# Loads of k and q issued two slots ahead, and GpSimd's last sums of w_a put behind VectorE's last sums of h

## The chip, the cores and the metric

The kernel runs on one core of one Trainium2 chip. The metric is the time of one execution on the device, in microseconds (us). Three runs of the kernel before took 219.48, 219.63 and 220.11 us; their median is 219.63 us.

## What is computed

Four batches of eight heads go through a decayed linear recurrence over 768 steps with heads of width 64, and its output, seen as 3072 tokens of width 512, goes through a bilinear feed-forward layer of width 1536:

```python
for t in range(S):
    state = gamma * state + einsum('bhd,bhe->bhde', k[:, :, t], v[:, :, t])
    y[:, :, t] = scale * einsum('bhd,bhde->bhe', q[:, :, t], state)
x = y.transpose(0, 2, 1, 3).reshape(B * S, H * D)
out = ((x @ w_a) * (x @ w_b)) @ w_out
```

Inputs and output are float32; the kernel multiplies in bf16 and sums in float32.

## The kernel before, in words

**Slots and blocks.** The 24 slots (four batches of six) are 128 steps each. For a slot, k and q are multiplied by tables of decays into one bf16 tile `kqb` (`scaled`, line 233), a DMA turns that tile over into `kqT` (line 256), and v is cast to bf16 into `vb` (line 264). From these, `turn` (line 411) makes on TensorE the state sums of two slots (`chunk_states`, line 281), their scores (`scores`, line 315) and the outputs of the two slots before (`inter`, `intra`), which ScalarE or VectorE copies into `xt`, the input of the feed-forward layer. The 3072 tokens go through that layer in eight blocks J of 4, 2, 2, 2, 2, 4, 4 and 4 slots (`TILES`, line 16). For each of twelve stripes `ft` of the width of 1536, TensorE makes a (`ffn_a`) and g (`ffn_g`), ScalarE copies a to bf16 (line 606), and VectorE multiplies the two into `ht` (line 617).

**Products with seven multiplications.** The product with w_out in J of 2 to 7 is made of seven products of halves where eight would be plain (`ffn_fast`, line 779, once for every two slots, so u = 0 and 1 in a block of four). It needs sums of parts of h, `hsum`, which `add` (line 664) makes: for each pair of stripes f four sums, numbered `which` 0 to 3. VectorE makes most of them. In J = 6 and 7 the product with w_a has this form as well, for f from 1 on (`seven_a`, line 719), and so needs sums of parts of x, `xs` (`combine_x`, line 678, on VectorE), and sums of parts of w_a, `ta` (`combine_a`, line 687, on GpSimd: four instructions for each f). In J = 6 the seven multiplications serve f of 1 to 3, in J = 7 f of 1 to 5. In J = 6 GpSimd also makes the sums of h of f up to 3 (`sums_of`, line 996), and VectorE those of f = 4 and 5 (`adds_of`), the last seven of them behind the last `ht`.

**Banks.** PSUM has three banks that a, g, the state sums and the products o share (`psff`, line 67). In `ffn_fast` the products R1, R2, R4 and R5 take banks from these three. R2 goes into the output by `plus` (line 791) on VectorE, and that instruction sets its bank free. Behind the three that R1, R2 and R4 hold, the state sums of a `turn` take the bank of R4, and R5 that of R2.

**Order of the work.** On every engine the order is that of the program: `seq` (line 75) ties each instruction to the one before it on its engine. What interleaves the slots with the blocks is a table written by hand, `ahead` (line 951): at the point (J, ft), (J, "o", i), (J, "mid") or (J, "sums", u) it calls `casts`, `turn` or `combine_a`, and `visit` (line 972) runs what stands there. Slots 6 to 23 go through `casts` (line 250): on GpSimd the two products with the tables and the cast of v, on SyncE's DMA queue (SP) the turning over and the loads that follow. SP issues DMAs one after the other, and one that waits holds up those behind it. The raw tiles of k, q and v hold two slots each and there are three of each kind; of `kqb`, `kqT` and `vb` there are six, so slot t takes over the tiles of slot t - 6. `store` (line 629) issues the outputs on SP, too. `combine_a` for f = 1, 2, 3 stands at (5, "sums", 0) behind the casts of slot 23, and for f = 4 and 5 in `sums_of` behind GpSimd's sums of h of J = 6, f = 3.

Of the kernel before, what the change touches and what calls it, by code (L numbers as in the profile page):

```python
# [12 lines left out]
ALU = mybir.AluOpType  # L13
# [14 lines left out]
def kernel(  # L28
# [10 lines left out]
    nc = tc.nc  # L39
# [8 lines left out]
    NSLOT = B * NCH  # L48
# [23 lines left out]
    last = {}  # L72
    nosync = mybir.DependencyInfo(mybir.DependencyClass.NoSync, mybir.DependencyReason.DATA)

    def seq(bi):
        ins = bi.ins
        prev = last.get(ins.engine)
        if prev is not None:
            tc.add_manual_dep(ins, prev.name, nosync, reason="program order")
        last[ins.engine] = ins  # L80
        return bi
# [4 lines left out]
    def load_slot(t, names="kqv"):  # L86
        b, ci = divmod(t, NCH)
        for nm in names:
            if t % 2 == 0:
                whole[nm] = raw.tile([P, 2, H, D], F32, tag=nm + "f", name=nm + "f")  # L90
            raws[nm, t] = whole[nm][:, t % 2]
            s = {"k": k, "q": q, "v": v}[nm][b, :, ci * P : (ci + 1) * P, :]
            if nm == "q":
                s = s.rearrange("h (n par) d -> par n h d", par=2)
                for par in range(2):
                    seq(nc.sync.dma_start(out=raws[nm, t][64 * par : 64 * par + 64], in_=s[par]))
            else:
                seq(nc.sync.dma_start(out=raws[nm, t], in_=s.rearrange("h p d -> p h d")))
# [101 lines left out]
    def cast(engine, dst, src):  # L200
        if engine is nc.scalar:
            seq(nc.scalar.copy(dst, src))  # L202
        else:
            seq(engine.tensor_copy(dst, src))  # L204
# [28 lines left out]
    def scaled(eng, t, i):  # L233
        ktab, qtab = tabs[0] if t < 2 * PAIRS else tabs[1]
        dst, src, tab = kqb[t][:, i], raws["kq"[i], t], (ktab, qtab)[i][:, t % NCH]
        dst = dst.rearrange("p hp r d -> p r hp d")
        src = src.rearrange("p (r hp) d -> p r hp d", r=2)
        tab = tab.rearrange("p (r hp) o -> p r hp o", r=2).to_broadcast([P, 2, HP, D])
        if t < 10:
            seq(eng.tensor_tensor(dst, src, tab, op=ALU.mult))  # L240
        else:
            for r in range(2):
                seq(eng.tensor_tensor(dst[:, r], src[:, r], tab[:, r], op=ALU.mult))  # L243

    def new_nat(t):
        kqb[t] = nat.tile([P, 2, HP, 2, D], BF16, tag="kqb", name="kqb")
        kb[t], qb[t] = kqb[t][:, 0], kqb[t][:, 1]
        vb[t] = nat.tile([P, H, D], BF16, tag="vb", name="vb")

    def casts(t, names="kqv"):  # L250
        if "k" in names:
            new_nat(t)
            scaled(nc.gpsimd, t, 0)
            scaled(nc.gpsimd, t, 1)
            kqT[t] = tra.tile([P, 2, HP, P], BF16, tag="kqT", name="kqT", bufs=6)
            seq(nc.sync.dma_start_transpose(
                out=kqT[t].rearrange("p a b c -> p (a b) c"),
                in_=kqb[t].rearrange("p a hp r d -> p (a hp r d)")))
            if t % 2 and t + 1 < NSLOT:
                for names in ("kq", "v"):  # L260
                    load_slot(t + 1, names)
                    load_slot(t + 2, names)
        if "v" in names:
            cast(nc.gpsimd, vb[t], raws["v", t])

# [13 lines left out]
    sums = {}  # L279
# [54 lines left out]
    after = mybir.DependencyInfo(mybir.DependencyClass.Sync, mybir.DependencyReason.DATA)  # L334
# [329 lines left out]
    def add(J, which, f0, f1, eng=nc.vector):  # L664
        if J not in hsum:
            hsum[J] = [wstage.tile([P, NH, 2, P], BF16, tag="w" + "ab"[i % 2], name="hsum") for i in range(4)]
        s = [x[:, f0:f1, : TILES[J] // 2] for x in hsum[J]]
        x, y, op = {
            0: (lambda: rows(J, 0, 1, f0, f1), lambda: rows(J, 1, 1, f0, f1), ALU.add),
            1: (lambda: s[0], lambda: rows(J, 0, 0, f0, f1), ALU.subtract),  # L670
            2: (lambda: rows(J, 0, 0, f0, f1), lambda: rows(J, 0, 1, f0, f1), ALU.subtract),
            3: (lambda: rows(J, 1, 0, f0, f1), lambda: s[1], ALU.subtract),
        }[which]
        seq(eng.tensor_tensor(s[which], x(), y(), op=op))  # L674
# [12 lines left out]
    def combine_a(f):  # L687
        if not ta:
            ta.extend(raw.tile([P, 2, NH, P], BF16, tag=t, name="ta") for t in ("kf", "kf", "qf", "qf"))
        w = wa_bf.rearrange("p (c k) (f r m) -> p c r f k m", c=2, r=2, m=P)  # L690
        b11, b12, b21, b22 = (w[:, c, r, f] for c in range(2) for r in range(2))
        t1, t2, t3, t4 = (t[:, :, f] for t in ta)
        for dst, x, y in ((t1, b12, b11), (t2, b22, t1), (t3, b22, b12), (t4, b21, t2)):
            seq(nc.gpsimd.tensor_tensor(dst, x, y, op=ALU.subtract))

    banks = {}

# [61 lines left out]
    behind = []  # L759
# [189 lines left out]
    for j in range(NO):  # L949
        cast_o(j)  # L950
    ahead = {
        (1, 6): [(casts, 6)], (1, 8): [(casts, 7)],
        (0, "o", 2): [(turn, 6, None), (casts, 8, "kq")],
        (0, "o", 3): [(casts, 9, "kq"), (casts, 8, "v"), (casts, 9, "v")],
        (1, "o", 1): [(turn, 8, 6, D_), (casts, 10)],
        (2, 2): [(casts, 11)], (2, 7): [(casts, 12)], (2, "o", 0): [(turn, 10, 8), (casts, 13)],
# [3 lines left out]
        (5, 0): [(casts, 20)], (5, 2): [(casts, 21)], (5, 3): [(turn, 16, None)],  # L960
        (5, 8): [(turn, 18, 16), (casts, 22)],
        (5, "sums", 0): [(turn, 20, 18), (casts, 23)],
        (6, 8): [(turn, 22, 20)], (6, "o", 0): [(turn, None, 22)],
    }
    ahead[5, "sums", 0] += [(combine_a, f) for f in (1, 2, 3)]
    early = {3: [(0, 0, 2)], 4: [(1, 0, 2)], 5: [(2, 0, 2)], 6: [(3, 0, 2)],
             7: [(0, 2, 4)], 8: [(1, 2, 4)], 9: [(2, 2, 4)], 10: [(3, 2, 4)]}
# [14 lines left out]
    def blocks_seven(J):  # L982
        f0, f1 = SEVEN[J]
        combine_x(J)
        store()
        for ft in range(2 * f0):
            ffn_a(J, ft)
        for f in range(f0, f1):
            seven_a(J, f)
            sums_of(J, f - 1)  # L990
            mask_now(1)
        seven_end(J, f1 - 1)
        sums_of(J, f1 - 1)
        return 2 * f1

    def sums_of(J, f):
        if J == 6 and f == 0:
            return
        if J == 6:
            f0, f1 = (0, 2) if f == 1 else (f, f + 1)  # L1000
            for which in range(4):
                add(J, which, f0, f1, nc.gpsimd)
            if f == 3:
                combine_a(4)
                combine_a(5)
        elif f < 5:
            for which in range(4 if f < 4 else 2):
                add(J, which, f, f + 1, nc.gpsimd)
        else:
            for which in range(2):  # L1010
                add(J, which, 5, 6)
            for which in (2, 3):
                add(J, which, 4, 6)
# [61 lines left out]
```

## Time and profile before

| | |
|---|---|
| median of three runs | 219.63 us |
| the profiled execution | 220.27 us |
| its span, first to last instruction | 218.6 us |
| TensorE busy | 211.2 us, 97% of the span |
| VectorE busy | 147.0 us, 67% |
| GpSimd busy | 120.7 us, 55% |
| ScalarE busy | 96.5 us, 44% |
| read from HBM, written to it | 28.31 MB, 6.29 MB |
| packets of SP's queue | 72.1% of 16 DMA engines' span |

Times in the views are in us from the start of the span, unless they are marked ns. PE is TensorE, DVE is VectorE, ACT is ScalarE, POOL is GpSimd and SP is SyncE. A row of the timeline gives the start, the duration, the engine, the line and the operation, the tiles written and read, and, in brackets, how long the engine was idle ahead of it and what ended that. Rows of several equal instructions one after the other are merged (x2 and so on). The ends of matmuls are modelled, so they are best read by their starts.

### The profile page before, as it was taken

The numbers are of one execution on the slowest core, as the hardware profiler recorded it, in microseconds if no ns is written. First come the engines' busy times: TensorE is split into PE (matmuls) and PEld (weight loads), VectorE is DVE, ScalarE is ACT, GpSimd is POOL, SyncE is SP. The second block draws the span as 40 slices with busy tenths as digits, with TensorE's granted clock in tenths as the row PEclk, the third lists the DMA queues.
The fourth block names the chain that finished last, engine by engine and source line by source line (L and its number), as shares of the span: only waits on it lengthen the run. The fifth ranks groups of instructions, "written<-read, shape, count | busy, mean of one in ns | idle before, by whom it ended". The sixth has DMA issues, their size and how long they took to land.

```text
span 218.6 us, 7060 instructions
## 1 busy us (share of the span) xinstructions
PE 211.2 (97%) x2875; PEld 155.8 (71%) x2875; DVE 147.0 (67%) x324; ACT 96.5 (44%) x240; POOL 120.7 (55%) x185
## 2 busy tenths in 40 slices
PE   8889999999999999999999999999999999999993
PEld 7568888886446888888878445488665487666682
DVE  1784456657926686699785387976887694777731
ACT  3675234442336436437464342736441742444231
POOL 6467789782745445155460544725999960087400
PEclk9999999999999999999999999999999999999999
DMA  6999999997999998899797879999610002200022
GB/s 169 345 372 382 371 313 396 352 221 167 220 263 253 228 248 98 123 232 196 174 153 176 224 138 235 195 204 185 200 43 3 3 0 99 97 0 4 0 96 96
DMA packets 94832, 39.77 MB, mean 182 GB/s; under 512 B 76112, under 2 KB 91728, under 8 KB 94800
## 3 DMA queue, kind: packets, MB, share of 16 engines
q1 hardware_dynamic: 94656, 39.20, 72.1%
q8 instruction: 22, 0.36, 0.7%
q10 hardware_dynamic: 144, 0.13, 0.2%
q14 instruction: 10, 0.08, 0.1%
HBM read 28.31 MB, written 6.29 MB: 158 GB/s over the span
## 4 chain that ended last, share of the span: by engine, by line
PE 86%; DVE 4%; DMA 3%; ACT 2%; POOL 1%; issue 1%; SPq 0%; DVEq 0%; POOLq 0%
PE g L614 27%; PE a L602 21%; PE o L776 17%; PE o L651 7%; PE a L716 6%; DMA kf<-in_k_dram 3%; DVE ht L617 2%; PE y L363 1%; POOL kqb L240 1%; PE at L321 1%; PE y L375 1%; PE st L291 1%; DVE hsum L674 1%; PE y L533 1%; PE tp L454 1%
## 5 line engine op out<-in xcount | busy, mean ns | idle before, releaser
L617 DVE TENSOR_TENSOR ht<-g,asb 128x256 bf16<-128x256 f32 (+1 forms) x98 | 53.8, 549 | 39.2 <-PE g L614 28.4
L614 PE MATMUL g<-xt,wb_bf 128*128 128x256 bf16 (+1 forms) x432 | 77.9, 308 | 0.4 <-ACT asb L606 0.4
L602 PE MATMUL a<-xt,wa_bf 128*128 128x256 bf16 (+1 forms) x368 | 60.9, 296 | 0.1
L606 ACT CAST asb<-a 128x256 bf16<-128x256 f32 (+1 forms) x82 | 36.8, 450 | 51.0 <-PE a L602 50.3
L614 PEld LDWEIGHTS <-wb_bf 128*128 128x128 bf16 x432 | 42.1, 98 | 16.8 <-issue 0.8
L602 PEld LDWEIGHTS <-wa_bf 128*128 128x128 bf16 x368 | 35.3, 98 | 12.3
L243 POOL TENSOR_TENSOR kqb<-kf,ktab 128x256 bf16<-128x256 f32 x28 | 17.1, 631 | 33.3 <-DMA kf<-in_k_dram 33.3
L204 POOL CAST vb<-vf 128x512 bf16<-128x512 f32 x24 | 14.7, 623 | 17.7 <-DMA vf<-in_v_dram 15.8
L776 PEld LDWEIGHTS <-hsum 128*128 128x128 bf16 x216 | 21.0, 98 | 2.7
L788 ACT COPY snap<-o 128x256 f32<-128x256 f32 x34 | 12.7, 374 | 20.2 <-PE o L776 20.1
L776 PE MATMUL o<-wt_bf,hsum 128*128 128x256 bf16 x162 | 19.4, 273 | 0.0
L674 POOL TENSOR_TENSOR hsum<-ht 128x256 bf16<-128x256 bf16 (+1 forms) x15 | 11.0, 732 | 15.0 <-DVE ht L617 15.0
L776 PEld LDWEIGHTS <-ht 128*128 128x128 bf16 x162 | 15.4, 98 | 3.1 <-issue 0.5
L243 POOL TENSOR_TENSOR kqb<-qf,qtab 128x256 bf16<-128x256 f32 x28 | 16.9, 622 | 1.2 <-DMA qf<-in_q_dram 1.2
L651 PE MATMUL o<-wo_bf,ht 128*128 128x512 bf16 x72 | 16.1, 380 | 0.0
L305 DVE TENSOR_TENSOR sums<-st,sums 128x256 f32<-128x256 f32 x30 | 12.7, 424 | 1.9 <-PE st L291 0.5
L776 PE MATMUL o<-wo_bf,ht 128*128 128x256 bf16 x108 | 13.3, 273 | 0.4 <-DVE osb L791 0.4
L202 ACT CAST gst<-sums 128x256 bf16<-128x256 f32 x33 | 12.6, 412 | 1.8 <-DVE sums L303 1.5
L240 POOL TENSOR_TENSOR kqb<-kf,ktab 128x512 bf16<-128x512 f32 x7 | 8.2, 1179 | 8.8 <-DMA kf<-in_k_dram 4.9
L674 DVE TENSOR_TENSOR hsum<-ht 128x256 bf16<-128x256 bf16 (+1 forms) x32 | 12.6, 397 | 0.3
L651 PEld LDWEIGHTS <-ht 128*128 128x128 bf16 x72 | 6.9, 98 | 7.9
L327 DVE TENSOR_TENSOR aT<-at,mask 128x512 bf16<-128x512 f32 x18 | 12.1, 681 | 0.0
(101 smaller groups left out, 276.1 us busy)
## 6 DMA issues: line engine op xcount, KB each, us to landing
out_dram<-osb SPq DMA_DIRECT2D x11, 512.0 KB, 3.5
kf<-in_k_dram SPq DMA_DIRECT2D x18, 256.0 KB, 3.9
qf<-in_q_dram SPq DMA_DIRECT2D x36, 128.0 KB, 3.9
vf<-in_v_dram SPq DMA_DIRECT2D x18, 256.0 KB, 4.1
wsta<-in_moe_w_a_dram SPq DMA_DIRECT2D x6, 512.0 KB, 7.8
wstb<-in_moe_w_b_dram SPq DMA_DIRECT2D x6, 512.0 KB, 7.7
wsto<-in_moe_w_out_dram SPq DMA_DIRECT2D x6, 512.0 KB, 8.2
kf<-in_k_dram SPq DMA_DIRECT2D x3, 512.0 KB, 6.3
```

The lines of the kernel that those rows point to most:

```text
L204: seq(engine.tensor_copy(dst, src))
L243: seq(eng.tensor_tensor(dst[:, r], src[:, r], tab[:, r], op=ALU.mult))
L305: seq(nc.vector.tensor_tensor(new, u[c][:, s], old, op=ALU.add))
L602: seq(nc.tensor.matmul(a[:, b0 - c0 : b1 - c0], wa_bf[:, kt, fs], xcols(J, kt, b0, b1), start=(kt == 0 and b0 == c0), stop=(kt == KT - 1 a ...
L606: seq(nc.scalar.copy(asb, a))
L614: seq(nc.tensor.matmul(g[:, b0 - c0 : b1 - c0], wb_bf[:, kt, fs], xcols(J, kt, b0, b1), start=(kt == 0 and b0 == c0), stop=(kt == KT - 1 a ...
L617: seq(nc.vector.tensor_tensor(ht[J][:, ft, c0:c1], g, asbs.pop((J, ft, c0)), op=ALU.mult))
L651: seq(nc.tensor.matmul(o, ht[J][:, ft, i * P : (i + 1) * P], wo_bf[:, f, 2 * r : 2 * r + 2, :].rearrange("p a d -> p (a d)"), start=(ft == ...
L674: seq(eng.tensor_tensor(s[which], x(), y(), op=op))
L716: seq(nc.tensor.matmul(R, w, x, start=(first and k == 0), stop=(k == 1), skip_group_check=True))
L776: seq(nc.tensor.matmul(R[:, :DH], lhs, (wo_bf, wt_bf)[w][:, f, m, :], start=(first and f == 0), stop=(f == NH - 1), skip_group_check=True))
L788: seq(nc.scalar.copy(snap[:, i], R[:, :DH]))
```

## The change

Three places. In `casts`, the loads of k and q of slot t + 2 are issued right behind the turning over of slot t, for even and odd t alike. Before, they were issued for two slots together behind the turning over of each odd slot: k and q of both, then v of both. The loads of v stay behind the odd slots. Second, `combine_a` for f = 4 and 5 moves from `sums_of` to the point (6, "sums", 1), which lies in the second `ffn_fast` of block 6. Third, the first instruction of each of these two calls waits for the last VectorE instruction issued up to that point.

```diff
             seq(nc.sync.dma_start_transpose(
                 out=kqT[t].rearrange("p a b c -> p (a b) c"),
                 in_=kqb[t].rearrange("p a hp r d -> p (a hp r d)")))
-            if t % 2 and t + 1 < NSLOT:
-                for names in ("kq", "v"):
-                    load_slot(t + 1, names)
-                    load_slot(t + 2, names)
+            if t + 2 < NSLOT:
+                load_slot(t + 2, "kq")
+                if t % 2:
+                    load_slot(t + 1, "v")
+                    load_slot(t + 2, "v")
...
         t1, t2, t3, t4 = (t[:, :, f] for t in ta)
+        wait = last[mybir.EngineType.DVE].name
         for dst, x, y in ((t1, b12, b11), (t2, b22, t1), (t3, b22, b12), (t4, b21, t2)):
-            seq(nc.gpsimd.tensor_tensor(dst, x, y, op=ALU.subtract))
+            bi = seq(nc.gpsimd.tensor_tensor(dst, x, y, op=ALU.subtract))
+            if f > 3 and dst is t1:
+                tc.add_manual_dep(bi.ins, wait, after, reason="behind VectorE's sums")
...
-        (6, 8): [(turn, 22, 20)], (6, "o", 0): [(turn, None, 22)],
+        (6, 8): [(turn, 22, 20)], (6, "o", 0): [(turn, None, 22)], (6, "sums", 1): [(combine_a, 4), (combine_a, 5)],
...
                 add(J, which, f0, f1, nc.gpsimd)
-            if f == 3:
-                combine_a(4)
-                combine_a(5)
```

## The prediction

> **What bounds the kernel now.** I read the page first, then the waits of TensorE, then the timelines of TensorE, VectorE and GpSimd around the two things that the change moves.
>
> ```profile
> span 218.6 us, 7060 instructions
> ...
> PE 211.2 (97%) x2875; PEld 155.8 (71%) x2875; DVE 147.0 (67%) x324; ACT 96.5 (44%) x240; POOL 120.7 (55%) x185
> ```
>
> TensorE is busy for 211.2 of 218.6 us. A change on other engines can only bring what TensorE loses by waiting, and it costs as soon as it adds a wait. The waits of TensorE from 40 us on, where the slots of the changed loop begin, are these (us in total, times, longest):
>
> ```profile
> PE o L776 <- DVE osb L791: 0.4, 1, 0.4
> PE g L614 <- ACT asb L606: 0.3, 1, 0.3
> ```
>
> Two waits, and no DMA, no `kqT` and no GpSimd among them. So the earlier loads free no wait of TensorE directly; what can be had is mainly the first row. Its place on TensorE (block J = 6, from u = 0 to u = 1), and below it a place of block 5 where nothing waits:
>
> ```profile
> 179.77 0.82 PE L776 MATMUL o<-wo_bf,hsum 128*128 128x256 bf16 x6
> 180.95 1.47 PE L776 MATMUL o<-wo_bf,ht 128*128 128x256 bf16 x12 [0.36 <-DVE osb L791]
> ```
>
> ```profile
> 143.97 0.82 PE L776 MATMUL o<-wt_bf,ht 128*128 128x256 bf16 x6
> 144.63 0.82 PE L776 MATMUL o<-wt_bf,hsum 128*128 128x256 bf16 x6
> ...
> 146.76 1.48 PE L776 MATMUL o<-wt_bf,hsum 128*128 128x256 bf16 x12
> ```
>
> Six such matmuls last 144.63 - 143.97 = 0.66 from start to start where nothing holds them. In block 6 the step is 180.95 - 179.77 = 1.18, so the wait costs 0.52. (The 0.36 in brackets is less, because ends are modelled.) The first product of u = 1 takes the bank that `plus`, line 791, sets free. Why that was late is seen on VectorE, in the same block:
>
> ```profile
> 175.97 0.37 DVE L674 TENSOR_TENSOR hsum<-hsum,ht 128x256 bf16<-128x256 bf16 x1
> ...
> 178.90 0.28 DVE L397 TENSOR_TENSOR xt<-y,part 128x128 bf16<-128x128 f32 x1
> ...
> 180.49 0.41 DVE L791 TENSOR_TENSOR osb<-o,snap 128x256 f32<-128x256 f32 x1
> ...
> 182.51 0.42 DVE L791 TENSOR_TENSOR osb<-o,snap 128x256 f32<-128x256 f32 x1 [0.69 <-ACT snap L788]
> ```
>
> The last seven sums of h take 178.90 - 175.97 = 2.93, then come eight small writes of `xt`, then line 791. Block 5 has the same seven sums in the same order, and goes from them straight to line 791:
>
> ```profile
> 142.94 0.69 DVE L617 TENSOR_TENSOR ht<-g,asb 128x512 bf16<-128x512 f32 x1 [0.50 <-PE g L614]
> 143.54 0.28 DVE L674 TENSOR_TENSOR hsum<-hsum,ht 128x256 bf16<-128x256 bf16 x1
> ...
> 145.08 0.42 DVE L791 TENSOR_TENSOR osb<-o,snap 128x256 f32<-128x256 f32 x1
> ```
>
> There they take 145.08 - 143.54 = 1.54. The difference of 1.39 goes with what GpSimd does at the time:
>
> ```profile
> 93.30 1.23 POOL L243 TENSOR_TENSOR kqb<-kf,ktab 128x256 bf16<-128x256 f32 x2 [5.21 <-DMA kf<-in_k_dram]
> ...
> 97.58 0.61 POOL L204 CAST vb<-vf 128x512 bf16<-128x512 f32 x1 [1.80 <-PE y L375]
> ...
> 154.54 0.85 POOL L694 TENSOR_TENSOR ta<-wa_bf 128x256 bf16<-128x256 bf16 x1
> ...
> 172.85 0.67 POOL L694 TENSOR_TENSOR ta<-wa_bf 128x256 bf16<-128x256 bf16 x1
> ...
> 177.71 0.71 POOL L694 TENSOR_TENSOR ta<-wa_bf,ta 128x256 bf16<-128x256 bf16 x1
> 191.05 0.67 POOL L674 TENSOR_TENSOR hsum<-ht 128x256 bf16<-128x256 bf16 x1 [12.62 <-DVE ht L617]
> ```
>
> From 172.85 to 178.42 it makes the eight sums of w_a of f = 4 and 5, one behind the other, 5.57 / 8 = 0.70 each, and these lie over VectorE's seven sums of block 6. Over those of block 5 lie none: the first sum of w_a starts at 154.54. So I take 1.39 as the price of seven VectorE sums beside GpSimd's sums of w_a.
>
> **Part one: the sums of f = 4 and 5 move.** Eight GpSimd instructions go from 172.85 to behind the last VectorE instruction of the program at (6, "sums", 1). That is line 791 of u = 1, the row of 182.51. VectorE's seven sums then take 1.54, and line 791 of u = 0 comes up to 1.39 earlier, for it waits for nothing else: its product was made long before. TensorE wants the bank 0.52 ahead of where it got it, so the wait goes whole: minus 0.52. Next late is nothing there, with 1.39 - 0.52 = 0.87 to spare.
>
> The added wait holds GpSimd up to about 182.4 (the 182.93 of the end of that row, less 0.52). Queued behind the waiting instruction are the seven other sums and then the sums of h of block 7, at 191.05. From 182.4 eight times 0.70 ends at 188.0; GpSimd was idle for 12.62 ahead of 191.05, so nobody waits, and f = 4 comes only as the fourth of block 7's seven-fold products. They now lie over `combine_x` of block 7. In block 6 `combine_x` also ran beside sums of w_a, which began at 154.54:
>
> ```profile
> 154.06 0.80 DVE L685 TENSOR_TENSOR xs<-xt 128x512 bf16<-128x512 bf16 x1 [0.78 <-POOL kqb L243]
> ```
>
> The list of TensorE's waits shows nothing there, so I cost this at nothing; were the cover gone, each of its four sums could cost what the seven paid, 1.39 / 7 = 0.2.
>
> **Part two: the loads.** One turn of the loop in SP's queue:
>
> ```profile
> 87.56 1.23 SPq L256 DMA_TRANSPOSE kqT<-kqb  x1
> 88.85 1.37 SPq L98 DMA_DIRECT2D kf<-in_k_dram  x1
> ...
> 93.89 1.67 SPq L98 DMA_DIRECT2D vf<-in_v_dram  x2
> ...
> 100.65 1.24 SPq L256 DMA_TRANSPOSE kqT<-kqb  x1
> ```
>
> At 87.56 slot 13 is turned over, at 100.65 slot 15: 13.1 for two slots. In between, GpSimd stands for 5.21 waiting for k of slot 14 and then until 97.58 for v, which was issued behind k and q of two slots. Though the bracket at 97.58 names TensorE, I take this wait as one for v, which is issued at 93.89, 3.69 earlier; the product that the bracket stands for, in block 2, was over long before. From 97.58 to 100.65 it is 3.07 to the next turning over.
>
> After the change, k and q of the even slot are issued half a turn earlier, so GpSimd no longer waits for them, and v stands behind k and q of one slot. The issues of two slots' k and q take 93.89 - 88.85 = 5.04 here, those of one 2.5, so v is issued 1.3 + 2.5 = 3.8 behind the odd turning over in place of 6.3. The loop becomes 3.8 + 3.69 + 3.07 = 10.6, or 2.5 less for every two slots. What is moved past: the turning over of an odd slot now stands behind three more issues in SP's queue, but it waits for GpSimd's products with that slot, which come 3.07 behind v anyway. A store between them comes no later than before. TensorE has no wait for `kqT` to lose or gain.
>
> Over the seven turns up to slot 23 this would put GpSimd some 17 ahead of the 154.54 at which its casts end, but the tiles stop it: `vb` of slot 22 takes the tile of slot 16, which TensorE reads last here:
>
> ```profile
> 135.34 0.48 PE L375 MATMUL y<-aT,vb 64*64 64x64 bf16 x32
> ```
>
> So the cast of v of slot 22 starts at 135.8 at the soonest. Behind it come the products of slot 23 (two of 1.2, as in the row of 93.30) and its cast (0.61): the sums of w_a of f = 1 to 3 begin between 139.4 and 154.5. I take 140.5, near the lower end, since 17 is more than the 15 between the two. Twelve of them at 0.70 last to 149. That window holds VectorE's sums of block 5, from before 143.54 to 145.08: the change takes GpSimd's sums of w_a off VectorE's in block 6 and pushes others onto VectorE's in block 5.
>
> What that costs: the seven sums become 1.39 longer, and three earlier ones of the block (the table of sums puts one behind stripe 9 and two behind stripe 10) may share the window; at the same rate they would add 0.6. The 0.50 of idle time at 142.94 swallows most of that, so I take line 791 as 1.8 later, between 1.4 and 2.0. It ended at 145.50. R5, the product of 146.76, takes its bank, so 1.26 are spare and the wait is 1.8 - 1.26 = 0.54. As to the ends: nothing, if GpSimd comes later than 145; 0.9, if the product of 144.63, which wants the first three sums, also waits two tenths or so.
>
> **A rule of the skill.** In block 6 the seven sums beside GpSimd's took 2.93, that is 0.42 for each, although GpSimd's instructions are 0.70 long. The Trainium skill, "SBUF — State Buffer", section "SBUF: two separate sides", says that VectorE with two inputs from SBUF and GpSimd hold a shared pair of ports in turn, each for its whole instruction, and that the other is blocked fully. By that rule each of the seven sums could stand behind a whole instruction of 0.70, and the sum below would be 221.6; the 2.93 of the trace agrees with the direction, not with the size.
>
> **The sum.** Minus 0.52 in block 6, plus 0.54 in block 5: nothing, within tenths. The profiled execution took 220.27, its span 218.6, so 1.7 lie around it and stay. It was 0.64 above the median of 219.63; as the sum is a difference, I put it on the median: 219.6. A measurement of this kernel can tell about 0.3% from no change, here 0.66.
>
> **The rivals.**
> - *The collision does not come* (GpSimd is slower to get ahead, because landings lengthen when the same bytes go in less time, so that the loads hardly do what they are for, or it falls into spare time). Then only part one counts: 219.63 - 0.52 = 219.1. For it: the wait for k did not show how long the loads take when nothing is spare. Against it: the 17 that the loop would gain. 0.22; a third of that I count as faster by the noise of the runs.
> - *Slower: block 5 becomes bound by VectorE.* If each of ten sums there pays half of a GpSimd instruction, 0.35, line 791 is 3.5 late less the 0.5 idle: the wait is 3.0 - 1.26 = 1.7, the time 219.63 - 0.52 + 1.7 = 220.8. It decides from the point where the wait is over 0.66 + 0.52 = 1.18, line 791 thus 2.4 late. For it: the row of 154.06, one VectorE sum of 0.80. Against it: the measured 2.93 for seven. If each of the seven waited out a whole GpSimd sum, they would take 7 x 0.70 = 4.9, 2.0 more than I take, and the time would be 221.6; this has 0.03 of the 0.15.
> - *Faster by more:* the other wait, for `asb`, goes as well, 0.3 by its row, and nothing comes in block 5: 219.63 - 0.52 - 0.3 = 218.8. Against it: nothing that is moved runs on ScalarE. 0.08.
>
> **How the numbers follow.** The forecast, both effects and nothing left, has 0.55, and its own range is 219.1 (no cost in block 5) to 220.0 (0.9). The rivals have 0.22, 0.15 and 0.08. The range of 218.9 to 220.4 holds the forecast, the first rival with the scatter of runs, and the low edge of the slower one. Faster by over 0.3%: 0.08 and 0.08, so 0.16. Slower: 0.15 and 0.02 from the forecast's edge, so 0.17. The same: 0.67.
>
> **What would show it.** In the changed profile: the sums of w_a of f = 4 start behind 182, VectorE's seven sums in block 6 take about 1.5, and TensorE's wait for line 791 at 180.95 is gone. GpSimd's waits for k, 5.21 at 93.30, shrink to one or two; its sums of w_a start near 140; the seven sums of block 5 take nearly 3; and TensorE waits near 147 for line 791. The prediction is wrong if these sums start behind 145, or if they lie over VectorE's and TensorE waits there for less than 0.1 or more than 1.2.

## The result: slower by about 1.1%

| | median | range | runs |
|---|---|---|---|
| before | 219.56 us | 219.39 to 220.11 | 4 |
| after | 222.17 us | 221.23 to 222.75 | 4 |

The ratio is 1.0111, with an interval of 1.0071 to 1.0150. (Some executions of these kernels take over 1.5% longer than their fastest, most of them at a lower granted clock; the ratios leave these out, five of nine runs of e6 and one of seven of e3 among them, so they need not be the quotient of two medians.) The forecast was 219.6 us within 218.9 to 220.4, so it was wrong, and on the slow side. The profiled execution of after took 222.15 us with a span of 220.4, 1.8 more than the span of before.

### The profile page after: what moved, and what is told of

Its sections match the earlier page's. It is cut to its first block, busy times and chain, and to the rows that moved or that the text cites. A ratio compares the mean times of both kernels' runs of the same rounds, so it can differ in the third digit from the quotient of the medians.

```text
span 220.4 us, 7059 instructions
## 1 busy us (share of the span) xinstructions
PE 212.1 (96%) x2871; PEld 156.3 (71%) x2875; DVE 150.1 (68%) x324; ACT 96.8 (44%) x240; POOL 121.2 (55%) x184
## 4 chain that ended last, share of the span: by engine, by line
PE 84%; DVE 7%; DMA 3%; issue 2%; ACT 2%; POOL 1%; SPq 0%; DVEq 0%; POOLq 0%; ACTq 0%
PE g L615 26%; PE a L603 21%; PE o L780 17%; PE o L652 7%; PE a L720 5%; DVE hsum L675 3%; DMA kf<-in_k_dram 3%; DVE ht L618 2%; POOL kqb L240 1%; PE at L322 1%; PE y L364 1%; PE y L376 1%; PE st L292 1%; ACT asb L607 1%; PE tp L455 1%
## 5 line engine op out<-in xcount | busy, mean ns | idle before, releaser
L204 POOL CAST vb<-vf 128x512 bf16<-128x512 f32 x23 | 14.1, 619 | 31.7 <-DMA vf<-in_v_dram 23.8
L675 DVE TENSOR_TENSOR hsum<-ht 128x256 bf16<-128x256 bf16 (+1 forms) x32 | 14.2, 448 | 0.3
L696 POOL TENSOR_TENSOR ta<-wa_bf 128x256 bf16<-128x256 bf16 x10 | 7.6, 760 | 10.4 <-DVE osb L795 10.4
```

## The profile after

The page's span and busy times, and then the waits of TensorE from 40 us on (us in total, times, longest):

```profile
span 220.4 us, 7059 instructions
...
PE 212.1 (96%) x2871; PEld 156.3 (71%) x2875; DVE 150.1 (68%) x324; ACT 96.8 (44%) x240; POOL 121.2 (55%) x184
```

```profile
PE o L780 <- DVE osb L795: 1.8, 2, 1.1
PE g L615 <- ACT asb L607: 0.3, 1, 0.3
```

Lines moved by a few: 776 became 780 and 791 became 795. VectorE is busy for 3.1 us more, though it does the same 324 instructions: that is the first sign that something lengthens them. TensorE's wait for line 795 was 0.4 once and is 1.8 in two places. Where they are, by the timeline of TensorE of after (start, duration, operation, in brackets the idle time and what ended it):

```profile
117.25 0.82 PE L780 MATMUL o<-wt_bf,hsum 128*128 128x256 bf16 x6
118.83 1.47 PE L780 MATMUL o<-wt_bf,hsum 128*128 128x256 bf16 x12 [0.77 <-DVE osb L795]
120.14 0.82 PE L780 MATMUL o<-wo_bf,hsum 128*128 128x256 bf16 x6
...
145.85 1.06 PE L780 MATMUL o<-wt_bf,hsum 128*128 128x256 bf16 x6
149.18 1.47 PE L780 MATMUL o<-wt_bf,hsum 128*128 128x256 bf16 x12 [1.06 <-DVE osb L795]
...
182.17 0.82 PE L780 MATMUL o<-wo_bf,hsum 128*128 128x256 bf16 x6
182.83 1.47 PE L780 MATMUL o<-wo_bf,ht 128*128 128x256 bf16 x12
```

In block 6 the step 182.17 to 182.83 is 0.66 where it was 1.18: the 0.52 is gone, as predicted. In block 5, R5 starts 149.18 - 145.85 = 3.33 behind the product ahead of it, where before it was 2.13. In block 4 there is a wait that before did not have; there the same two products ran on without a gap, as the timeline of before shows in one row (x18 instead of x6 and x12):

```profile
117.14 2.13 PE L776 MATMUL o<-wt_bf,hsum 128*128 128x256 bf16 x18
```

VectorE of after at these two places, and in block 6:

```profile
115.27 0.70 DVE L675 TENSOR_TENSOR hsum<-ht,hsum 128x256 bf16<-128x256 bf16 x1
...
118.37 0.41 DVE L795 TENSOR_TENSOR osb<-o,snap 128x256 f32<-128x256 f32 x1
...
144.34 0.68 DVE L618 TENSOR_TENSOR ht<-g,asb 128x512 bf16<-128x512 f32 x1
144.94 0.28 DVE L675 TENSOR_TENSOR hsum<-hsum,ht 128x256 bf16<-128x256 bf16 x1
...
148.72 0.41 DVE L795 TENSOR_TENSOR osb<-o,snap 128x256 f32<-128x256 f32 x1
...
178.37 0.28 DVE L675 TENSOR_TENSOR hsum<-hsum,ht 128x256 bf16<-128x256 bf16 x1
...
179.91 0.28 DVE L398 TENSOR_TENSOR xt<-y,part 128x128 bf16<-128x128 f32 x1
```

VectorE of before at the last five sums of block 4:

```profile
115.63 0.28 DVE L674 TENSOR_TENSOR hsum<-ht,hsum 128x256 bf16<-128x256 bf16 x1
...
116.75 0.42 DVE L791 TENSOR_TENSOR osb<-o,snap 128x256 f32<-128x256 f32 x1
```

And GpSimd of after over the same times:

```profile
115.07 0.76 POOL L204 CAST vb<-vf 128x512 bf16<-128x512 f32 x1 [4.95 <-DMA vf<-in_v_dram]
115.79 1.27 POOL L243 TENSOR_TENSOR kqb<-kf,ktab 128x256 bf16<-128x256 f32 x2
...
140.42 0.85 POOL L696 TENSOR_TENSOR ta<-wa_bf 128x256 bf16<-128x256 bf16 x1
...
148.60 0.71 POOL L696 TENSOR_TENSOR ta<-wa_bf,ta 128x256 bf16<-128x256 bf16 x1
...
184.90 0.67 POOL L696 TENSOR_TENSOR ta<-wa_bf 128x256 bf16<-128x256 bf16 x1 [10.37 <-DVE osb L795]
```

Reading the two side by side: in block 4 GpSimd now makes the products of slot 19 (four instructions from 115.79 to 118.3, two with k and two with q), and VectorE's last five sums take 118.37 - 115.27 = 3.10, or 0.62 each, where before they took 116.75 - 115.63 = 1.12, or 0.22 each. In block 5 the sums of w_a of f = 1 to 3 run from 140.42 to 149.3 and VectorE's seven sums take 148.72 - 144.94 = 3.78, where before it was 1.54. In block 6 nothing of GpSimd lies beside them and the seven take 1.54.

The sum, by the starts on TensorE: R5 of block 5 starts 149.18 - 146.76 = 2.42 later than before. Of this, 0.97 was there already at the start of the block (0.1 from earlier, and 0.85 from block 4, by the product behind the wait: it starts at 120.14, in before at 119.18), and 1.45 comes in block 5: 3.33 - 2.13 = 1.20 at R5, and 0.25 in the first product of the block, whose 12 matmuls (not among the rows here) take 145.19 - 143.63 = 1.56 where they took 143.97 - 142.66 = 1.31. Then 0.52 is won in block 6. That is 1.9, and the spans differ by 1.8.

## The experiments

**The theory after the result.** The mechanism of the forecast is right: VectorE's sums stretch where GpSimd works beside them. Its extent was not: ordinary products with the tables do it too, in block 4, and more of the sums are held up than I took. **Rivals:** the cost comes from the sums of f = 4 and 5 in their new place; or from the DMAs, in that earlier loads hold up what stands behind them in SP's queue. Expectations are printed as they stood before the run.

**1. The sums alone**, the loads as before, and **2. the loads alone**, the sums as before:

```diff
 e1_sums_only, against the kernel after
-            if t + 2 < NSLOT:
-                load_slot(t + 2, "kq")
...
+            if t % 2 and t + 1 < NSLOT:
+                for names in ("kq", "v"):
...
 e2_loads_only: the first hunk of the change and nothing else
```

> The second and third edit alone: the loads as before, the sums of w_a of f = 4 and 5 moved and held back. Theory A (GpSimd's work, pushed forward by the early loads, lies over VectorE's sums of blocks 4 and 5 and lengthens them): TensorE's wait of 0.52 in block 6 goes and none comes, 0.5 faster than before, 219.1. Theory B (the early loads themselves crowd SP's queue, so that a store or a landing is late and holds VectorE's line of the output): the same 219.1. Theory C (the added wait and the new place of the eight sums cost what was lost): 1.5 to 2.5 slower than before, 221 to 222.

> The first edit alone: loads of k and q two slots ahead, the sums of w_a of f = 4 and 5 in their old place. Theories A and B: the waits of 0.85 in block 4 and 1.45 in block 5 are there, and that of 0.5 in block 6 comes back: about 0.5 slower than the changed kernel, 222.7. Theory C: as fast as before, 219.6.

The loads alone: ratio 1.0114, 1.0085 to 1.0143, all of the change's loss; that they would be 0.5 slower than after, for want of block 6's gain, did not come true. The sums alone: 0.9999, 0.9984 to 1.0013. So the loss is the loads', and the second and third place of the change cost nothing that can be told. They bring nothing either: TensorE's waits in the trace of the sums alone are down to one row, so the 0.5 of block 6 is gone there, but the median shows no gain, against what I expected.

```profile
PE g L614 <- ACT asb L606: 0.3, 1, 0.3
```

**3. Before, two more executions**, to see why:

> The kernel before, for a second profile. If the second edit's 0.5 is missing from the medians because most executions of the kernel before do not have the wait of 0.5 in block 6, this one lacks it; if it stands here too, the gain is real in the trace and is lost among the scatter elsewhere.

> The same kernel and question once more: the wait of 0.5 in block 6 stands, or not.

The first (219.99 us) has the wait in block 6 again, 0.3 by its row. The second (220.11 us) has a wait of 0.6 for line 791 in block 5 instead, and none in block 6. VectorE in block 5 of this second execution, and GpSimd beside it:

```profile
144.19 1.32 DVE L674 TENSOR_TENSOR hsum<-ht 128x256 bf16<-128x256 bf16 x2
145.43 1.32 DVE L674 TENSOR_TENSOR hsum<-ht,hsum 128x256 bf16<-128x256 bf16 x2
146.67 0.41 DVE L791 TENSOR_TENSOR osb<-o,snap 128x256 f32<-128x256 f32 x1
```

```profile
143.99 1.37 POOL L243 TENSOR_TENSOR kqb<-kf,ktab 128x256 bf16<-128x256 f32 x2 [3.92 <-DMA kf<-in_k_dram]
145.32 1.28 POOL L243 TENSOR_TENSOR kqb<-qf,qtab 128x256 bf16<-128x256 f32 x2
```

Four sums take 146.67 - 144.19 = 2.48, 0.62 each, beside four products of 0.64 to 0.69. So k of that slot landed a little earlier than in the other execution (GpSimd starts at 143.99 and not at 146.36), and the kernel before has this very collision by itself. Which block it falls on changes from one execution to the next. All three profiled executions of before have one such wait, and all three (219.99 to 220.27) lie above its median of 219.56 in the result; that the usual execution has none, and so nothing for the moved sums to win, would fit, but no trace shows it.

**4. Part of the collision taken away.** In the first kernel f = 1 to 3 wait for VectorE's last instruction too; in the second the products of slot 19 wait so as well, which keeps them off block 4:

```diff
 e3_ta_behind, against the kernel after
-            if f > 3 and dst is t1:
+            if dst is t1:
 e4_both_behind, against e3_ta_behind
...
+                if t in held_by:
+                    tc.add_manual_dep(bi.ins, held_by.pop(t), after, reason="behind VectorE's sums")
...
+            if t == 19:
+                held_by[t] = last[mybir.EngineType.DVE].name
```

> The changed kernel, and the first GpSimd sum of w_a of f = 1 to 3 also waits for the last VectorE instruction issued at its point, which lies behind the seven sums of block 5. Theory A: those seven sums take 1.5 in place of 3.8, TensorE's wait of 1.45 in block 5 goes, that of block 4 stays: 222.2 - 1.45 = 220.7. Theory B: nothing changes, since loads and stores are as in the changed kernel: 222.2.

> The kernel of the run before, and GpSimd's products of slot 19 also wait for the last of VectorE's sums of block 4. Theory A: the wait of 0.85 in block 4 goes as well, but for one or two tenths from the cast of v of slot 18, which still lies over one or two sums: 219.9 to 219.1, with loads as early as in the changed kernel up to slot 18. Theory B: 222 still.

Ratios 1.0057 (1.0036 to 1.0079) and 1.0050 (1.0024 to 1.0076). Holding f = 1 to 3 back takes 1.0111 - 1.0057 = 0.0054 off, 1.2 us, give or take 0.0045 by the two intervals: block 5's collision. In the profile of e3 the seven sums of block 5 are back at 1.53, and no wait for line 795 is left. Holding slot 19 as well brought nothing that can be told, and e3's profile shows a reason: GpSimd's cast of v of slot 18 began only at 117.29 there, and the products behind it missed VectorE's sums without being held. (That v landed late is likely, but the bracket of that row names TensorE.) What remained, 0.5% in both, was something else, the rival of SP's queue after all. A wait of TensorE in e3; e4 has the same one with 0.8:

```profile
PE at L322 <- DMA kqT<-kqb: 1.2, 1, 1.2
```

It is for `kqT` of slot 9, at 65 us in block 1, where the forecast had no wait to lose. SP's queue of before and of after at that place:

```profile
56.71 2.54 SPq L256 DMA_TRANSPOSE kqT<-kqb  x1
59.35 0.52 SPq L631 DMA_DIRECT2D out_dram<-osb  x1
59.97 1.58 SPq L256 DMA_TRANSPOSE kqT<-kqb  x1
```

```profile
55.26 2.90 SPq L256 DMA_TRANSPOSE kqT<-kqb  x1
58.20 0.58 SPq L98 DMA_DIRECT2D kf<-in_k_dram  x1
58.83 1.30 SPq L96 DMA_DIRECT2D qf<-in_q_dram  x2
60.23 0.57 SPq L632 DMA_DIRECT2D out_dram<-osb  x1
60.90 1.70 SPq L256 DMA_TRANSPOSE kqT<-kqb  x1
```

Slot 8 is turned over, then slot 9. Before, only a store lay between; after, k and q of slot 10 lie between too. GpSimd's product with q of slot 9, in before and in after:

```profile
58.78 1.04 POOL L240 TENSOR_TENSOR kqb<-qf,qtab 128x512 bf16<-128x512 f32 x1 [0.79 <-DMA qf<-in_q_dram]
```

```profile
57.52 1.41 POOL L240 TENSOR_TENSOR kqb<-qf,qtab 128x512 bf16<-128x512 f32 x1 [0.84 <-DMA qf<-in_q_dram]
```

In before, slot 9 waited for this product, which ended at 59.82; in after it was done at 58.93, and the turning over stood in the queue until 60.90.

**5. Slot 10 alone.** The first kernel is e4 with k and q of slot 10 behind the turning over of slot 9, all other loads early. The second is before, with only k and q of slot 10 ahead of it:

```diff
 e5_slot10_behind, against e4_both_behind
-                load_slot(t + 2, "kq")
+                if t == 9:
+                    load_slot(t + 1, "kq")
+                if t != 8:
+                    load_slot(t + 2, "kq")
 e6_slot10_ahead, against the kernel before
+            if t == 8:
+                load_slot(t + 2, "kq")
...
+                    if (t, names) != (9, "kq"):
+                        load_slot(t + 1, names)
-                    load_slot(t + 1, names)
```

> The kernel with both groups of GpSimd's work held back, and k and q of slot 10 go back behind the turning over of slot 9; all other loads stay early. Theory D (what was left, about 0.9, is TensorE's wait for kqT of slot 9 at 65 us, because three more DMA issues stand ahead of its turning over): that wait goes, no DMA is left among TensorE's waits, and the time is that of the second and third edit alone, 219.7. Theory B (early loads cost all along the loop): 220.5 as without this edit.

> The kernel before, with one edit: k and q of slot 10 are issued ahead of the turning over of slot 9, as the change does; every other load and all sums as before. Theory D: TensorE waits for kqT of slot 9 at 65 us, by 0.1 to 1.3, and the time is 0.1 to 1.2 above the kernel before: 219.9 to 220.9. If the queue's order costs nothing: 219.7 and no such wait.

With slot 10 behind, the ratio is 1.0013 (0.9992 to 1.0035): no loss clear of the noise is left, though k and q of seven other slots are still loaded earlier than before. With slot 10 alone ahead it is 1.0099 (1.0056 to 1.0141), and TensorE waits 2.0 for `kqT`. The wait and the loss were both more than expected (up to 1.3, and up to 1.2 us where 1.0099 is 2.2), so the place was right and the size was not. By these ratios the loss of after splits into 0.54% for block 5's sums of w_a (after to e3), 0.07% for slot 19's products (e3 to e4), which is nothing that can be told, and 0.37%, give or take 0.34%, for slot 10's loads (e4 to e5).

Over the profiles of before, after and the experiments with loads moved, the wait follows the issue of slot 9's turning over, while TensorE comes to it at 64.9 to 65.6 each time (the wait is the step from the first half of the scores to the second, less some 0.15 that the first half takes):

| kernel | turning over issued | second half of the scores starts | wait by starts |
|---|---|---|---|
| before | 59.97 | with the first | 0 |
| e5 | 60.20 | with the first | 0 |
| after | 60.90 | with the first | 0 |
| e2 | 61.35 | 65.67 | 0.6 |
| e3 | 61.64 | 66.47 | 1.3 |
| e4 | 61.89 | 66.51 | 1.0 |
| after, again | 62.59 | 67.25 | 2.1 |
| e6 | 62.85 | 67.64 | 2.2 |

From issue to use it takes 4.3 to 4.8 wherever TensorE waited. So before had about 1 us to spare here, and the first profiled execution of after still came through without a wait.

**6. After, a second execution**, since the first profile shows no such wait:

> The changed kernel, for a second profile. Theories A and D together: the waits of 0.85 in block 4 and 1.45 in block 5 stand again within 0.3, and that for kqT of slot 9 is what differs between executions, between 0 and 1.3. Span 220 to 221.5.

It took 224.51 us, above all four runs of the result (221.23 to 222.75), and its span of 222.8 is outside what was expected. TensorE's timeline and one window of that execution (length; busy time of PE, PEld, DVE, ACT and POOL; the granted clock; DMA):

```profile
65.03 0.32 PE L322 MATMUL at<-kqT 64*64 64x64 bf16 x16
67.25 0.32 PE L322 MATMUL at<-kqT 64*64 64x64 bf16 x16 [1.90 <-DMA kqT<-kqb]
67.91 4.45 PE L652 MATMUL o<-wo_bf,ht 128*128 128x512 bf16 x11
72.20 0.60 PE L603 MATMUL a<-xt,wa_bf 128*128 128x256 bf16 x4
```

```profile
67.50:71.50 4.00, 3.94 (x63) 1.79 (x51) 1.29 (x2) 2.29 (x6) 0.50 (x1) 0.60 0.89 212
```

The wait of 2.1 is there. Behind it the granted clock is 0.60, and the product with w_out takes 72.20 - 67.91 = 4.29 where after's first profile has 2.60: another 1.7. Block 4's wait is absent in this execution, against what was expected; block 5's is 1.4. There the cast of v of slot 22 waited for its landing until 144.20, so that the products of slot 23 lay over the first of VectorE's sums, and the sums of w_a, from 148.08, over the rest. So the costs of the change come in different shares from one execution to the next.

**7. Idle GpSimd work beside block 4's sums**, with the loads as before. In all three kernels idle instructions are added to e1 whose result nobody uses: six subtractions behind the start of block 4's product, six copies (one input) in their place, and eight subtractions starting earlier and writing two tiles in turn:

```diff
 e7_idle_two_inputs, against e1_sums_only
...
+        for i in range(6):
+            bi = seq(nc.gpsimd.tensor_tensor(idle_out, wb_bf[:, 0:2, :P], wb_bf[:, 2:4, :P], op=ALU.subtract))
...
+    ahead[4, "o", 0].insert(0, (idle_work,))
 e8_idle_one_input, against e7_idle_two_inputs
-            bi = seq(nc.gpsimd.tensor_tensor(idle_out, wb_bf[:, 0:2, :P], wb_bf[:, 2:4, :P], op=ALU.subtract))
+            bi = seq(nc.gpsimd.tensor_copy(idle_out, wb_bf[:, 0:2, :P]))
 e9_idle_earlier, against e7_idle_two_inputs
...
+        for i in range(8):
+            bi = seq(nc.gpsimd.tensor_tensor(idle_out[:, i % 2], wb_bf[:, 0:2, :P], wb_bf[:, 2:4, :P], op=ALU.subtract))
...
+    ahead[4, 11] = [(idle_work,)]
```

> The second and third edit alone (loads as before), and at block 4 GpSimd does six subtractions of two bf16 tiles of 128x256 into a tile that nobody reads, started by VectorE's fourth of the eight sums there. No load or DMA is touched. Theory A: VectorE's next four sums go at GpSimd's pace, about 0.62 each in place of 0.23, so line 791's successor there is 1.5 late, of which 0.6 are spare: a wait of about 0.9 at 118 us, 220.5. Theory B: nothing, 219.7.

> As the run with six subtractions, but six copies of one bf16 tile of 128x256. If it is any GpSimd work over the sums that counts: sums as long as a copy and a wait of some tenths. If only work that reads two tiles counts (the cast of v of slot 18 lay over a sum and lengthened it by less than 0.1): sums of 0.2 to 0.3, no wait, 219.7.

> As the run with six subtractions, but eight of them, started two sums earlier and written to two tiles in turn, so that GpSimd leaves no gap between them. Loads as before. Theory A: VectorE's six sums behind the last ht of block 4 each wait for a whole GpSimd instruction, 0.62 to 0.67 each in place of 0.23, so line 791's successor there ends 2 to 2.5 late, 0.6 of it spare: TensorE waits 1.4 to 1.9 at 118 us for VectorE, and the time is about 1.2 above the kernel before, 221.0. Theory B (loads and landings are what costs): no wait there, 219.7.

The six subtractions gave 0.9998 (0.9978 to 1.0017): a miss. They began over the last four sums only, two of these lengthened, to 0.66 and 0.75, and line 794 came 117.34 - 116.75 = 0.59 later than in before, within the 0.6 or so that block 4 has to spare there. (Later casts shifted with it, and its profile has a wait of 0.4 in block 5.) The copies gave 0.9999 (0.9972 to 1.0025); beside them the same four sums took 1.21 against 0.93 in e1. The eight that began earlier gave 1.0073 (1.0053 to 1.0093), near what was expected. VectorE of that kernel, and its GpSimd:

```profile
115.54 0.75 DVE L674 TENSOR_TENSOR hsum<-ht,hsum 128x256 bf16<-128x256 bf16 x1
...
118.91 0.41 DVE L794 TENSOR_TENSOR osb<-o,snap 128x256 f32<-128x256 f32 x1
```

```profile
114.80 5.34 POOL L973 TENSOR_TENSOR idle_out<-wb_bf 128x256 bf16<-128x256 bf16 x8 [0.23 <-DVE hsum L674]
```

Five sums take 118.91 - 115.54 = 3.37, 0.67 each, and one GpSimd instruction takes 5.34 / 8 = 0.67. TensorE waits 0.5 for the sums and 1.3 for line 794. (This profiled execution, 222.85 us, is the slowest of the ten; their median is 221.31.) Subtractions on GpSimd beside block 4's sums, without a gap from the first sum on, are thus enough for a loss, 0.7% here, with no load moved. Whether copies placed as early would do the same was not tried.

## Why the prediction was wrong, point by point

- **Part one, minus 0.52 in block 6: right in the trace, to the hundredth.** The sums of f = 4 begin at 184.90, behind 182; the seven sums take 1.54; TensorE's step is 0.66. In e2, where these sums stay put, they reach over three of the seven, line 792 comes 0.88 late, and TensorE just does not wait, which bears out the 0.87 to spare. What failed is taking the 0.52 to the median: the sums alone gave 0.9999. The sums that moved lie over `combine_x` of block 7, which now takes 190.90 - 187.97 = 2.93 where it took 187.76 - 186.09 = 1.67, and TensorE does not wait for it, as costed.
- **Part two, GpSimd gets ahead: right in the first profile.** From 60 to 155 us, GpSimd's waits for k fall from 33.3 to 5.5, while those for v rise from 14.9 to 22.8. Two slots take 11.0 on average where they took 13.3 (13.1 to 10.6 by the forecast). The cast of v of slot 22 waits for TensorE, as forecast, and the sums of w_a were put at 140.5 and began at 140.42. In the second profile they began at 148.08, so the exact hit is partly luck.
- **Part two, the price in block 5: mis-sized, and this is the term of the sum that failed.** The seven sums were to take 2.93 and took 3.78; the wait was to be 0.54 and was 1.45. The cost was carried over from block 6, 1.39 for seven sums, as if it were a rate. VectorE's seven sums in block 6 of before, behind the first (175.97, 0.37 long, in the prediction), and in block 5 of after, behind the first (144.94, 0.28 long, further up):

```profile
176.27 0.28 DVE L674 TENSOR_TENSOR hsum<-ht 128x256 bf16<-128x256 bf16 x1
176.58 0.64 DVE L674 TENSOR_TENSOR hsum<-hsum,ht 128x256 bf16<-128x256 bf16 x1
177.14 1.43 DVE L674 TENSOR_TENSOR hsum<-ht 128x256 bf16<-128x256 bf16 x2
178.50 0.48 DVE L674 TENSOR_TENSOR hsum<-ht,hsum 128x256 bf16<-128x256 bf16 x2
```

```profile
145.14 0.75 DVE L675 TENSOR_TENSOR hsum<-ht 128x256 bf16<-128x256 bf16 x1
145.92 0.64 DVE L675 TENSOR_TENSOR hsum<-hsum,ht 128x256 bf16<-128x256 bf16 x1
146.49 0.95 DVE L675 TENSOR_TENSOR hsum<-ht 128x256 bf16<-128x256 bf16 x2
147.36 1.43 DVE L675 TENSOR_TENSOR hsum<-ht,hsum 128x256 bf16<-128x256 bf16 x2
```

In block 6 three sums are held up, to 0.64 and twice about 0.7; the first two come nearly or wholly free, between GpSimd's instructions, and the last two start at 178.50, when GpSimd's last sum has ended at 178.42. So 1.39 was the price of three sums held and not of seven. In block 5 GpSimd works on to 149.3, and five of the seven are held. That makes 3.78 - 1.54 = 2.24, which is 0.85 more than 1.39 and nearly all of 1.45 - 0.54 = 0.91. In block 4 and in e9 all five are held, at 0.62 and 0.67 each. The Trainium skill, "SBUF — State Buffer", section "SBUF: two separate sides", has VectorE and GpSimd hold a shared pair of ports in turn, each for its whole instruction. That agrees with the size of a held sum (GpSimd's instructions are 0.64 in block 4, 0.67 in e9 and 0.73 from start to start in block 5); it is too much only where it is charged to every one of the seven.

- **What was not priced: block 4, plus 0.85.** I went by the sums of w_a only, and by one block, though the row of 93.30 and its like were in the trace: the ordinary products are GpSimd work as well, about 0.6 each. A GpSimd that gets ahead by a slot moves all of its work, over all of the blocks between.
- **"The turning over of an odd slot now stands behind three more issues in SP's queue, but it waits for GpSimd's products with that slot, which come 3.07 behind v anyway": wrong at slot 9**, and with it "TensorE has no wait for `kqT` to lose or gain". This was argued from the steady turn at 87 to 100, where the products of an odd slot stand behind the cast of v of the slot before. For slots 8 and 9 the table `ahead` has the products of both first and the casts of v behind them, so slot 9's products do not wait for v, and the queue is what its turning over waits for. A list of waits does not show that a transfer without a wait has only about 1 us to spare. This costs from 0 to 2.2, and up to 1.7 more where the clock was lower behind it; e6 shows that this one position can cost 1% by itself, and e5 that without it, and with both collisions held off, no loss clear of the noise is left.
- **The rivals.** The slower one, block 5 bound by VectorE, had the right sign, place and mechanism, and 0.15 of the chance; it turned at a wait of 1.18, and 1.45 was measured. Even so it gave 220.8, for block 4 and slot 9 were in no case of mine.

In sum, the forecast was -0.52 + 0.54. The first profile has -0.52 + 1.45 + 0.85 + 0.1 = 1.9, and the wait for slot 9 comes on top in other executions.

What stays open: how much block 4 costs in a usual execution, since e3 and e4 do not separate it, and what makes k of a slot land earlier in one execution than in another. No version beat the kernel before: e1 and e5 are level with it.

## What to carry to other kernels

When an engine off the critical path is made to run ahead, list everything that it then does beside each stage that has little to spare, not only the piece the change is about, and count how many instructions can be held up there, each by how much, and do not carry over the mean of one place. When DMAs are issued earlier, go through the queue at the first turn of the loop as well as at a steady one, and ask of each transfer that is passed how much time its consumer has to spare, which a list of waits does not tell. Take profiles of several executions of the kernel before: which of two near-critical collisions happens can change between them.

## What the runs showed of the hardware

**Behind waits of 2 us on TensorE its clock was lower.** Behind waits of 2.1 (after, again) and 2.2 (e6) the granted clock was 0.60 and 0.57 from 67.5 to 71.5, and the product with w_out took up to 4.29 / 2.60 = 1.65 times as long. In e9, where waits of 0.5 and 1.3 lie within 2 us, the clock was 0.75 from 120 to 126. Behind a wait of 1.3 in the same place (e3) the clock stayed at 1.00, as behind those of block 4 and 5 in after, where the step behind R5's start was 120.14 - 118.83 = 1.31. The Trainium skill, "TensorE: Matmul & The Clock Gate", section "HAM oscillation — how this bites in real kernels", warns of gaps above about 3.4 us; here the clock was lower behind 2.1. That the wait causes the lower clock is read from its place, and was not tried apart.

**Not every VectorE instruction stretches beside GpSimd.** The product with g from PSUM at 144.34 takes 0.68 amid GpSimd's sums, as it took 0.69 in before with none; the sums with both inputs from SBUF are the ones that stretch. Six short GpSimd copies, with one input, did little to them: 1.21 for four sums in e8, against 1.78 beside the subtractions of e7 and 0.93 with neither. But one input is no safeguard: in after, the sum at 115.27 took 0.70 beside the cast of v of 115.07, which lasted 0.76.
